# Double blocks with one PSUM tile per bank, gate and value half products in turns, and one listed order for blocks 1 to 8

## The chip, the cores and the metric

The kernel runs on one core of one Trainium2 chip. The engines named below are PE (matrix multiply), PEld (its weight loads), DVE (vector), ACT (scalar activations and copies), POOL (GpSimd) and SP, whose queue issues nearly all DMAs. Every engine works through its own instructions in their order and stops at one whose inputs or room are not there yet. The metric is the device time in microseconds of one execution, the median of several runs.

## The reference

```python
def _attn_ref(q, k, v):                 # (8, 8, 576, 64): batch, heads, positions, head size
    scores = scale * np.matmul(q, k.transpose(0, 1, 3, 2))
    mask_local = (rel >= 0) & (rel < stride)                       # stride 32, heads 0..3
    mask_strided = (rel >= 0) & (pos[None, :] % stride == pos[:, None] % stride)   # heads 4..7
    ...
    attn = np.exp(scores)
    attn = attn / (np.sum(attn, axis=-1, keepdims=True) + 1e-09)
    return np.matmul(attn, v).astype(np.float32)

def _moe_ref(x, w_gate, w_val, w_out):  # x (4608, 512), w_gate and w_val (512, 1536), w_out (1536, 512)
    gate = 1.0 / (1.0 + np.exp(-(x @ w_gate)))
    val = x @ w_val
    return (gate * val @ w_out).astype(np.float32)
```

The attention's output, its heads side by side, is the `x` of the gated layer.

## The kernel before

**Blocks.** The 4608 tokens are nine blocks of 512: for each of the 8 batches the first 512 positions (blocks 0 to 7), and the last 64 of all batches together (block 8). Attention is done in pieces, four for each batch: local heads and strided heads, two times two. A piece is a row of small matmuls for the scores (`score`), mask, maximum, subtraction (`soft`), `expo` on ACT, sum and scaling (`norm`), eight 32-row transposes on DVE (`turn_blocks`), and small matmuls with the values (`weigh`), whose result is copied out of PSUM (`split_high`, `split_low`, `keep_raw`, `keep_rest`). The pieces of batches 2 to 7 are done while the gated layer of earlier blocks runs. Tiles of a piece (`qk`, `vv`, `sb`, `mx`, `pt`) are there once, so one piece is in work at a time.

**The gated layer.** The 1536 inner columns are 12 groups `f` of 128. All float32 values are split into a high and a low part, and each product is three matmuls (high by high, high by low, low by high). For blocks 0, 1 and 2 a group is 12 matmuls of 128x128 by 128x512 for the gate (`g`), 12 for the value (`v`), sigmoid on ACT, product and the two parts on DVE and ACT, and 12 matmuls for the output (`glu_out`), which accumulate over the 12 groups in four banks.

**Double blocks.** Blocks 3 and 4, 5 and 6, 7 and 8 are done in twos (`superblock`, L653), with a scheme of seven products in place of eight. A pair of groups `q` has seven half products for the gates (G1 to G7) and seven for the values (V1 to V7), six matmuls each (L695). Products 1, 6, 7 and 4 are added up in one bank ("a", `to = a`), and after 1, 6 and 7 ACT copies the running sum out (L713) before the next may be added. Products 2, 5 and 3 go to the other bank ("d"), which DVE adds to the copies (L721). Sigmoids follow on ACT (L723, L728), products on DVE (L725, L731), and the hidden values of the second block are kept. Then the output products of the second block run alone, while the seven combinations of the next two blocks' inputs are built (`build_x`: POOL differences, an ACT cast and a DVE subtraction for each). The combinations of the weights are made once, in block 1 (`sum_sets`: six POOL instructions, ACT cast, DVE subtraction, two DMAs), kept in DRAM (`sets`), and come back through a ring of tiles with room for twelve half products (`load_group`).

**PSUM.** Eight banks: `g` and `v` of one bank each, `a`, `o0` and `o1` of two banks each. In double blocks 3 and 7 the gates use `g` and `v`, the values the two halves of the one tile `a`; in double block 5 the gates use the two halves of `o0` and the values those of `o1` (L654). Scores go to `g` and `v` and the values' products of a piece to `a`, or the other way round.

**Order.** Block 0 is listed by hand for all engines (`ORDER`, under `tc.manual_schedule()`). For blocks 1 to 8 only PE has the order in which the program is written (`tc.manual_schedule(engines={PE})`); a planner orders DVE, ACT, POOL and SP by what is ready in its own model of time. PE's order in a pair of groups is `SOFAR` or a variant of it:

```python
SOFAR = "G1 G2 G6 G5 G7 V1 V2 G4 G3 V6 V5 V7 A V4 V3 B"
END = "G1 G2 G6 G5 G7 V1 V2 G4 G3 V6 V5 V7 A Xg V4 Sg V3 B"
```

A and B are the output products of earlier groups, X and S the values and the scores of attention pieces.

Of the kernel before, what the change touches and what calls it, by code (L numbers as in the profile page):

```python
# [52 lines left out]
SOFAR = "G1 G2 G6 G5 G7 V1 V2 G4 G3 V6 V5 V7 A V4 V3 B"  # L53
EARLY = "G1 Xv G2 Sv G6 G5 G7 V1 V2 G4 G3 V6 V5 V7 A Xg V4 Sg V3 B"
MIDDLE = "G1 G2 G6 G5 G7 V1 V2 G4 G3 V6 Xg V5 Sg V7 A V4 V3 B"
FIRST = "G1 G2 G6 Xv G5 Sv G7 V1 V2 G4 G3 V6 V5 V7 A V4 V3 B"
END = "G1 G2 G6 G5 G7 V1 V2 G4 G3 V6 V5 V7 A Xg V4 Sg V3 B"
PLANS = {3: [EARLY, MIDDLE, FIRST] * 2, 5: [END] * 4 + [SOFAR] * 2, 7: [SOFAR] * PAIRS}

# [26 lines left out]
y10 l11.1 X13 s11 a11.2 g11.1 H13 b11.2 L13 R13 w11.2 O10 m11 u11.2 l11.2 x11 y11  # L86
"""
# [6 lines left out]
def attention_then_glu(ctx, tc, qk_l, qk_s, v_l, v_s, w_all, consts, out):  # L94
# [79 lines left out]
    def pair(b, step, space):  # L174
# [52 lines left out]

        def soft():
            sc = todo["soft"]
            prob, row, by_row = rows()  # L230
            if local:
                to = tiles["sb"][:, : 2 * ns * kk].rearrange("p (j n) -> p j n", j=2)
                for j, x in enumerate(sc):
                    heads = to[:, j : j + x.shape[1]]
                    nc.vector.tensor_tensor(heads, x, mask_l.broadcast_to([P, x.shape[1], ns * kk]), op=ALU.add)
            else:
                for j in range(2):
                    sv = sc[j % len(sc)][:, j // len(sc)].rearrange("p (t k) -> p t k", k=kk)
                    nc.vector.tensor_tensor(prob[:, j * ns : (j + 1) * ns], sv, mask_s.broadcast_to([P, ns, kk]), op=ALU.add)  # L239
            nc.vector.tensor_reduce(row, prob, axis=AX.X, op=ALU.max)  # L240
            nc.vector.tensor_tensor(prob, prob, by_row, op=ALU.subtract)
# [5 lines left out]
        def norm():  # L247
            prob, row, by_row = rows()
            nc.vector.tensor_reduce(row, prob, axis=AX.X, op=ALU.add)
            nc.vector.tensor_scalar_add(row, row, 1e-9)  # L250
            nc.vector.reciprocal(row, row)
            nc.vector.tensor_tensor(prob, prob, by_row, op=ALU.mult)

# [13 lines left out]
        def turn_blocks():  # L267

            tiles["pt"] = pt = space.tile([P, 2 * SS * QB], F32, tag="pt", name=f"pt{b}_{step}")
            src, dst = (x[:, : 2 * ns * QB].rearrange("p (t k) -> p t k", k=QB) for x in (tiles["sb"], pt))  # L270
            for n in range(P // LB):
                for h in range(2):
                    to, rows, col = (n // 2 * 2 + h) * LB, n * LB, n % 2 * LB
                    nc.vector.transpose(dst[to : to + LB, :, col : col + LB], src[rows : rows + LB, :, h * LB : (h + 1) * LB])  # L274
# [76 lines left out]
        def keep_rest():  # L351
# [6 lines left out]
            L=split_low, R=keep_rest, K=keep_raw,  # L358
        )

    def banks(tag, name):
        if tag in "gv":
            return [ps.tile([P, BANK], F32, tag=tag, name=name)]
        two = bank(tag, name)
        return [two[:, :BANK], two[:, BANK:]]

    def bank(tag, name):
        return ps.tile([P, 2 * BANK], F32, tag=tag, name=name)
# [63 lines left out]
    def glu_val(k, f, v=None):  # L432
        if v is None:
            v = ps.tile([P, BANK], F32, tag="v", name=f"v{k}_{f}")
            products(v, k, f, 1)
        e = hs[k, f]
        t = work.tile([P, TB], F32, tag="t", name=f"t{k}_{f}") if k == 0 else e
        hh, hl = parts_tiles(k, f)
        def high():
            nc.scalar.copy(hh, t)  # L440

        def low():
            nc.vector.tensor_tensor(hl, t, hh.bitcast(F32), op=ALU.subtract)

        nc.vector.tensor_tensor(t, e, v, op=ALU.mult)  # L445
        if k == 0:
            return high, low
        high(), low()
# [33 lines left out]
    def glu_out(k, *fs):  # L482

        if fs[0] == 0:
            acc[k] = [x for n in ("agv" if k in (4, 5, B) else ("o0", "o1")) for x in banks(n, f"o{k}_{n}")]
        for i in (0, 2, 1, 3) if k == B else range(NTT):
# [15 lines left out]
    ps = ctx.enter_context(tc.tile_pool(name="ps", bufs=1, space=bass.MemoryType.PSUM))  # L502
    dram = ctx.enter_context(tc.tile_pool(name="dram", bufs=1, space=bass.MemoryType.DRAM))
# [4 lines left out]
    pairs = {(b, p): pair(b, p, first if b == 0 and p % 2 else work) for b in range(2) for p in range(4)}  # L508
    products_of = {}
    parts = {}  # L510

    def step(what):

        kind, of = what[0], what[1:]
        if kind in "QVZSFENTPXHLR":
# [6 lines left out]
            pairs[b, p][kind](*args)  # L522
# [36 lines left out]
    sets = {}  # L559
# [3 lines left out]

    def spare(tag, name, dt):
        return work.tile([P, 4, P], dt, tag=tag, name=name)

    def plain_sets(q):
        sets[q] = dram.tile([P, 2 * 7, 2, 2, P], F32, name=f"sets{q}")
        for i in range(2):
            for n, w in ((0, wh), (1, wl)):  # L570
                a, b = (w[f][i].bitcast(F32).rearrange("p (k c m) -> p k c m", k=2, c=2) for f in (2 * q, 2 * q + 1))
                tc.keep_in_program_order(nc.sync.dma_start(sets[q][:, 7 * i : 7 * i + 2, n], a))
                tc.keep_in_program_order(nc.sync.dma_start(sets[q][:, 7 * i + 2, n], b[:, 1]))

    def sum_sets(q, i, c):
        n = (q * 2 + i) * 2 + c
        u = spare(("t", "h0")[n % 2], f"sum{q}_{i}_{c}", F32)
        for at, f in ((0, 2 * q), (2, 2 * q + 1)):
            nc.gpsimd.tensor_tensor(u[:, at : at + 2], part(wh[f][i], c), part(wl[f][i], c), op=ALU.add)
        for to, x, y, op in ((3, 2, 3, ALU.add), (2, 0, 2, ALU.subtract), (0, 3, 0, ALU.subtract), (1, 1, 0, ALU.subtract)):  # L580
            nc.gpsimd.tensor_tensor(u[:, to], u[:, x], u[:, y], op=op)
        h = spare("l0", f"sumh{q}_{i}_{c}", F32R)
        nc.scalar.copy(h, u)
        nc.vector.tensor_tensor(u.bitcast(F32R), u, h.bitcast(F32), op=ALU.subtract)
        nc.sync.dma_start(sets[q][:, 7 * i + 3 : 7 * i + 7, 0, c], h.bitcast(F32))
        nc.sync.dma_start(sets[q][:, 7 * i + 3 : 7 * i + 7, 1, c], u)

    units = [(k, q, u) for k in SUPER for q in range(PAIRS) for u in SOFAR.split() if u not in "AB"]
    groups, ring, left = [], {}, {}
    while sum(len(g) for g in groups) < len(units):  # L590
# [286 lines left out]
```

## Time and profile before

| | us |
|---|---|
| median of 3 runs | 1135.92 |
| lowest and highest of them | 1131.89, 1137.14 |
| the profiled execution: its time | 1141.66 |
| the profiled execution: first to last instruction (span) | 1139.8 |

The mean granted clock of TensorE over the span was 0.96 of full speed. In the views, an instruction's row gives its line, engine, what it writes and reads, and behind "idle before" how long its engine had nothing to do and what ended that. PE's and PEld's rows are two sides of the same work. A matmul's record lasts longer than the distance to the next one, since matmuls are pipelined.

### The profile page before, as it was taken

The numbers are of one execution on the slowest core, as the hardware profiler recorded it, in microseconds if no ns is written. First come the engines' busy times: TensorE is split into PE (matmuls) and PEld (weight loads), VectorE is DVE, ScalarE is ACT, GpSimd is POOL, SyncE is SP. The second block draws the span as 40 slices with busy tenths as digits, with TensorE's granted clock in tenths as the row PEclk, the third lists the DMA queues.
The fourth block names the chain that finished last, engine by engine and source line by source line (L and its number), as shares of the span: only waits on it lengthen the run. The fifth ranks groups of instructions, "written<-read, shape, count | busy, mean of one in ns | idle before, by whom it ended". The sixth has DMA issues, their size and how long they took to land.

```text
span 1139.8 us, 18423 instructions
## 1 busy us (share of the span) xinstructions
PE 985.1 (86%) x7624; PEld 772.5 (68%) x7624; DVE 604.6 (53%) x981; ACT 429.7 (38%) x754; POOL 122.9 (11%) x188
## 2 busy tenths in 40 slices
PE   5998988788799887799889898779788998999998
PEld 4786777667578665577667686556556786777776
DVE  6877846555666685567546752544323633222242
ACT  4877743323433343344333532223222422222221
POOL 0000044575200111000000120000000300000000
PEclk9998999998898897999999999899899999999999
DMA  7665645666512143555445404344333315434311
GB/s 253 205 198 175 190 161 176 203 199 185 166 55 72 55 137 108 179 189 174 141 129 170 148 19 143 115 138 126 94 109 113 109 44 153 137 112 148 110 37 37
DMA packets 85027, 154.13 MB, mean 135 GB/s; under 512 B 5840, under 2 KB 40016, under 8 KB 84944
## 3 DMA queue, kind: packets, MB, share of 16 engines
q1 hardware_dynamic: 83024, 146.72, 40.7%
q10 hardware_dynamic: 1920, 6.24, 1.7%
q8 instruction: 60, 0.98, 0.4%
q14 instruction: 23, 0.19, 0.1%
HBM read 121.48 MB, written 31.46 MB: 134 GB/s over the span
## 4 chain that ended last, share of the span: by engine, by line
PE 46%; DVE 12%; ACT 7%; issue 1%; DMA 0%; POOL 0%; ACTq 0%; DVEq 0%
PE V_a L695 9%; PE o_o L455 8%; PE G_o L695 6%; PE G_g L695 5%; PE V_o L695 4%; PE o_a L455 4%; DVE pt L274 4%; PE G_v L695 3%; PE o_v L455 2%; PE o_g L455 2%; DVE e L721 1%; DVE h L731 1%; ACT e L723 1%; PE x L305 1%; ACT h L713 1%
## 5 line engine op out<-in xcount | busy, mean ns | idle before, releaser
L455 PE MATMUL o_o<-w,hh 128*128 128x512 f32 x576 | 179.2, 392 | 0.0
L695 PE MATMUL V_a<-xs,ring 128*128 128x512 f32 x504 | 133.8, 404 | 31.7 <-DVE h L731 9.8
L695 PEld LDWEIGHTS V_a<-xs,ring 128*128 128x128 f32 x504 | 91.9, 189 | 65.9 <-ACT hid L713 14.3
L455 PEld LDWEIGHTS o_o<-w,hh 128*128 128x128 f32 x576 | 107.8, 189 | 23.1
L418 PE MATMUL g<-xh,w 128*128 128x512 f32 x256 | 95.2, 433 | 27.1 <-DVE sb L239 12.6
L455 PE MATMUL o_o<-w,hl 128*128 128x512 f32 x288 | 112.3, 390 | 0.0
L274 DVE STREAM_TRANSPOSE pt<-sb 32x320 f32<-32x320 f32 (+1 forms) x192 | 102.9, 536 | 3.2
L695 PE MATMUL G_o<-xs,ring 128*128 128x512 f32 x252 | 74.9, 442 | 28.8 <-DVE e L721 15.6
L418 PE MATMUL v<-xh,w 128*128 128x512 f32 x256 | 88.9, 407 | 4.2 <-DVE e L445 4.1
L695 PEld LDWEIGHTS G_o<-xs,ring 128*128 128x128 f32 x252 | 51.0, 211 | 50.2 <-DVE e L721 18.2
L418 PEld LDWEIGHTS g<-xh,w 128*128 128x128 f32 x256 | 53.0, 207 | 42.5 <-DVE sb L239 13.6
L695 PE MATMUL V_o<-xs,ring 128*128 128x512 f32 x252 | 66.3, 402 | 10.8 <-ACT h L713 4.3
L695 PE MATMUL G_g<-xs,ring 128*128 128x512 f32 x288 | 74.3, 393 | 0.0
L695 PE MATMUL G_v<-xs,ring 128*128 128x512 f32 x216 | 58.7, 409 | 8.1 <-DVE e L721 8.1
L695 PEld LDWEIGHTS V_o<-xs,ring 128*128 128x128 f32 x252 | 46.1, 190 | 26.6 <-ACT h L713 6.8
L455 PEld LDWEIGHTS o_o<-w,hl 128*128 128x128 f32 x288 | 54.1, 188 | 12.1 <-DVE hl L738 0.4
L695 PEld LDWEIGHTS G_g<-xs,ring 128*128 128x128 f32 x288 | 54.0, 189 | 12.3 <-ACT e L713 0.6
L418 PEld LDWEIGHTS v<-xh,w 128*128 128x128 f32 x256 | 50.3, 197 | 16.7 <-DVE e L445 5.7
L723 ACT ACTIVATE e<-e 128x512 f32<-128x512 f32 x54 | 34.1, 632 | 72.9 <-DVE e L721 72.8
L199 POOL MEMSET sb<- 128x120 f32 x16 | 3.2, 200 | 527.3 <-DVE pt L274 397.1
L721 DVE TENSOR_TENSOR e<-e,G_v 128x512 f32<-128x512 f32 x36 | 24.6, 684 | 61.1 <-PE G_v L695 31.9
L418 PE MATMUL g<-xl,w 128*128 128x512 f32 x128 | 54.1, 422 | 0.0
(137 smaller groups left out, 1666.4 us busy)
## 6 DMA issues: line engine op xcount, KB each, us to landing
ring<-sets SPq DMA_DIRECT2D x126, 512.0 KB, 3.8
raw<-in_w_all SPq DMA_DIRECT2D x36, 512.0 KB, 4.3
qk<-in_qk_s SPq DMA_DIRECT2D x14, 599.0 KB, 5.5
vv<-in_v_l SPq DMA_DIRECT2D x13, 640.0 KB, 4.8
qk<-in_qk_l SPq DMA_DIRECT2D x14, 592.0 KB, 5.0
out<-ob SPq DMA_DIRECT2D x32, 256.0 KB, 2.0
sets<-w SPq DMA_DIRECT2D x24, 256.0 KB, 3.2
sets<-sumh SPq DMA_DIRECT2D x24, 256.0 KB, 2.4
```

Of the source, the lines that this page charges most:

```text
L199: nc.gpsimd.memset(sb[:, : 2 * ns * QB].rearrange("p (t k) -> p t k", k=QB)[:, :, GS:], 0.0)
L274: nc.vector.transpose(dst[to : to + LB, :, col : col + LB], src[rows : rows + LB, :, h * LB : (h + 1) * LB])
L305: nc.tensor.matmul(at_bank(r, (u * per + g) * m, (u * per + g + 1) * m)[j * D : (j + 1) * D], v[rows, (u * per + g) * P + j * D : (u * per ...
L418: nc.tensor.matmul(o, w, x, start=first and n == 0, stop=last and n == len(todo) - 1)
L455: nc.tensor.matmul(acc[k][i], h[:, i * P : (i + 1) * P], w, start=f == 0 and n == 0, stop=f == NF - 1 and n == 2,)
L695: nc.tensor.matmul(to, w[:, (wi * 2 + c) * P : (wi * 2 + c + 1) * P], x[xi][:, c], start=p in "125" and c == j == 0, stop=c == 1 and j == ...
L713: nc.scalar.copy(got[m, p], a)
L721: nc.vector.tensor_tensor(x, x, d, op=ALU.add)
L723: nc.scalar.activation(x, x, AF.Sigmoid)
L731: nc.vector.tensor_tensor(x, got["G", "4"], a, op=ALU.mult)
```

## The change

All instructions of blocks 1 to 8 are listed, for all engines, in one string `REST_ORDER`, whose entries a table `STEPS` maps to small functions; the plans, `begin_attention`, `scores`, `out_next` and `superblock` go. `ORDER` and block 0 stay. The larger functions are cut into steps (mask, maximum, subtraction and so on) that the list can place one by one. Besides the order:

- The two-bank tile `a` exists during block 0 only. After it, `a0` and `a1` are tiles of one bank each. In all three double blocks the gates use `g` and `v`, the values `a0` and `a1`, and `o0` and `o1` hold the outputs of blocks 1, 2, 3, 5 and 7; those of 4, 6 and 8 are in `g`, `v`, `a0`, `a1`.
- The half products come in the order G1 V1 G2 V2 G6 V6 G5 V5 G7 V7 G4 V4 G3 V3. A ring load brings the gate's and the value's set of one product together.
- Score and value matmuls of a piece stand between pairs of groups; pieces 18 and 19 are taken up in the output stage of block 4 and not in the double block.
- The weight sums are spread over blocks 1 and 2; every other cast has a tile of its own (`ost`).
- A new ACT instruction, `expo_first`, computes an exponential of one column ahead of each piece's `expo`.
- The second of the four input differences runs on DVE and not on POOL. An output row tile's eviction (`e`) and store (`d`) are steps of their own.

```diff
-SOFAR = "G1 G2 G6 G5 G7 V1 V2 G4 G3 V6 V5 V7 A V4 V3 B"
...
+REST_ORDER = """
+LQ0 g1.0 pa0.0.0 LV0 pb0.0.0 pl0 v1.0 s1.0 pa0.0.1 o0.11 pb0.0.1 m1.0 e0.0 x1.0 d0.0 e0.1 y1.0 d0.1 S0.0 LQ1 M0.0 M0.1 D0 g1.1 A0 U0 E0 v1.1 N0 s1.1
+W0 e0.2 e0.3 g1.2 d0.2 m1.1 d0.3 B0.0 x1.1 y1.1 v1.2 B0.1 s1.2 B0.2 ph0.0.0.1 ph0.0.1.0 B0.3 o1.0 m1.2 Z1 pw0.0.0 x1.2 y1.2 pd0.0.0 pw0.0.1 X0.0
...
+ph3.1.1.0 M6.1 A6 D6 U6 pb4.0.0 pl4 g2.3 xh3.0.2 pw3.1.1 E6 xl3.0.2 pd3.1.1 ph4.0.0.1 N6 v2.3 W6 s2.3 B6.0 B6.1 oh2.2.0 B6.2 B6.3 m2.3 Z7 X6.0 pw4.0.0
...
+M14.0 M14.1 D14 A14 U14 G3.2.1 E14 N14 V3.2.1 c3.2.0.1 W14 G3.2.2 r17 c3.2.1.1 B14.0 V3.2.2 B14.1 ad3.2.0.2 G3.2.6 r18 ad3.2.1.2 sg3.2.2 B14.2 V3.2.6
+B14.3 c3.2.0.6 G3.2.5 c3.2.1.6 mu3.2.2 Z15 x3.4 V3.2.5 y3.4 G3.2.7 r19 V3.2.7 c3.2.0.7 ad3.2.0.7 G3.2.4 r20 c3.2.1.7 sg3.2.7 ad3.2.1.7 V3.2.4 mu3.2.7
+sg3.2.4 G3.2.3 r21 mu3.2.4 x3.5 V3.2.3 ad3.2.0.3 y3.5 sg3.2.3 o3.3 r22 ad3.2.1.3 mu3.2.3 X14.0 S15.0 LV15 H14 R14 o3.4 LQ16 M15.0 M15.1 D15 A15 U15
...
+o4.8 x4.10 y4.9 y4.10 X19.1 x4.11 y4.11 S20.1 LV20 H19 o4.9 xh5.1.3 xd5.1.1 LQ21 R19 M20.0 xd5.1.2 xh5.1.6 M20.1 A20 D20 xh5.1.7 xl5.1.6 ob4 xl5.1.7
+xd5.1.3 U20 e4.0 xl5.1.3 xh5.1.4 d4.0 E20 xl5.1.4 e4.1 N20 d4.1 e4.2 G5.0.1 d4.2 W20 B20.0 V5.0.1 c5.0.0.1 e4.3 B20.1 G5.0.2 d4.3 r40 c5.0.1.1 B20.2
...
+"""
...
+        def expo_first():
+            mx = tiles["mx"]
+            nc.scalar.activation(mx[:, 14:15], ident[:, :1], AF.Exp)
...
+    def one_bank(tag, name):
+        return (ps if tag in "gv" else ps_b).tile([P, BANK], F32, tag=tag, name=name)
 
     def bank(tag, name):
-        return ps.tile([P, 2 * BANK], F32, tag=tag, name=name)
+        return (ps_a if tag == "a" else ps).tile([P, 2 * BANK], F32, tag=tag, name=name)
...
+    first_banks.close()
+    ps_b = ctx.enter_context(tc.tile_pool(name="ps_b", bufs=1, space=bass.MemoryType.PSUM))
...
+        (nc.vector if n == 1 else nc.gpsimd).tensor_tensor(t, x, y, op=ALU.subtract)
...
+    def half_product(k, q, m, p):
+        if p == 1:
+            two[m, 0] = one_bank("ga"[m] + "0" * m, f"p{m}{k}_{q}")
+        if p == 2:
+            two[m, 1] = one_bank("va"[m] + "1" * m, f"d{m}{k}_{q}")
+        to = two[m, int(p in (2, 5, 3))]
+        w = ring[k, q, str(p)][:, m]
...
+    STEPS = dict(
+        g=gate, v=val, o=glu_out, oh=lambda k, f, h: glu_out(k, f, half=(h,)), ob=lambda k: glu_out(k, NF - 2, NF - 1),
+        s=lambda k, f: sigmoid(k, f, products_of[k, f, 0]), m=lambda k, f: gated(k, f, products_of[k, f, 1]), x=split_high_h, y=split_low_h,
+        e=evict, d=store, LQ=load_queries, LV=lambda n: piece[n]["V"](), Z=lambda n: piece[n]["Z"](), S=score, M=masks,
...
+        pl=plain_sets, pa=sum_words, pb=sum_parts, ph=sum_high, pw=sum_low, pd=store_sums, r=load_group,
+        G=lambda k, q, p: half_product(k, q, 0, p), V=lambda k, q, p: half_product(k, q, 1, p), c=keep_sum, ad=add_sum, sg=gate_sigmoid,
+        mu=gate_times, xd=diff, xh=set_high, xl=set_low, z=rest_raw,
+    )
+    with tc.manual_schedule():
+        for what in REST_ORDER.split():
+            kind = what.rstrip("0123456789.")
+            STEPS[kind](*(int(n) for n in what[len(kind) :].split(".") if n))
```

In the list, A, U, E, N, W and B are a piece's maximum, subtraction, exponential, sum, scaling and a quarter of its transposes; H, L and R copy its result out of PSUM; `c` is the copy of a running sum, `ad` DVE's addition, `sg` a sigmoid, `mu` a product, `x` and `y` the high and low part of hidden values; `oh` is half of an output group, `ob` two groups at once.

More of the change, by code (lines that the diff above doesn't have):

```diff
@@ L507, in attention_then_glu @@
     left_over(0)
-    pairs = {(b, p): pair(b, p, first if b == 0 and p % 2 else work) for b in range(2) for p in range(4)}
+    firsts = {(b, p): pair(b, p, first if b == 0 and p % 2 else work) for b in range(2) for p in range(4)}
     products_of = {}
-    parts = {}
     def step(what):
@@ L557, in attention_then_glu, with load_queries, score, masks @@
                 left_over(1)
-    sets = {}
+    first_banks.close()
+    ps_b = ctx.enter_context(tc.tile_pool(name="ps_b", bufs=1, space=bass.MemoryType.PSUM))
+    todo = [(b, p) for b in range(BY_PE, B) for p in range(4)]
+    piece = {}
+    def load_queries(n):
+        piece[n] = pair(*todo[n], work)
+        piece[n]["Q"]()
+    def score(n, late):
+        if late:
+            piece[n]["S"](bank("o1", f"s{n}"))
+        else:
+            piece[n]["S"](*(one_bank(t, f"s{n}_{t}") for t in "gv"))
+    def masks(n, j):
+        if piece[n]["local"] and j == 0:
+            piece[n]["Z"]()
+        piece[n]["M"](j)
+    def values(n, late):
+        if late:
+            piece[n]["X"](bank("o0", f"x{n}"))
+        else:
+            piece[n]["X"](*(one_bank(t, f"x{n}_{t}") for t in ("a0", "a1")))
+    def high_of(n):
+        b, p = todo[n]
+        if p == 0:
+            (x_tiles if b < SUPER[0] else raw_tile)(b)
+        if b < SUPER[0]:
+            piece[n]["H"]()
+        else:
+            piece[n]["K"](x_raw[b])
+    def rest_of(n):
+        b, p = todo[n]
+        if p == 0:
+            left_over(b)
+        piece[n]["R"]()
+    def gate(k, f):
+        products_of[k, f, 0] = one_bank("g", f"g{k}_{f}")
+        products(products_of[k, f, 0], k, f, 0)
+    def val(k, f):
+        products_of[k, f, 1] = one_bank("v", f"v{k}_{f}")
+        products(products_of[k, f, 1], k, f, 1)
+    def evict(k, i):
+        give_out(k, i)
+    def store(k, i):
+        nc.sync.dma_start(out[k * S + i * P : k * S + (i + 1) * P], given[k, i])
+    sets, sums, sums_h = {}, {}, {}
     def part(w, c):
         return w.bitcast(F32).rearrange("p (k c m) -> p k c m", k=2, c=2)[:, :, c, :]
-    def spare(tag, name, dt):
-        return work.tile([P, 4, P], dt, tag=tag, name=name)
     def plain_sets(q):
@@ L585, in sum_sets @@
         nc.sync.dma_start(sets[q][:, 7 * i + 3 : 7 * i + 7, 0, c], h.bitcast(F32))
         nc.sync.dma_start(sets[q][:, 7 * i + 3 : 7 * i + 7, 1, c], u)
[L588 to L592 removed]
+    duos = [(k, q, p) for k in SUPER for q in range(PAIRS) for p in USE]
```

517 lines of the change are left out of this document (234 added, 283 removed).

## The prediction

> **What bounds the kernel now.** I read the page first.
>
> ```profile
> span 1139.8 us, 18423 instructions
> PE 985.1 (86%) x7624; PEld 772.5 (68%) x7624; DVE 604.6 (53%) x981; ACT 429.7 (38%) x754; POOL 122.9 (11%) x188
> L695 PE MATMUL V_a<-xs,ring 128*128 128x512 f32 x504 | 133.8, 404 | 31.7 <-DVE h L731 9.8
> L695 PE MATMUL G_o<-xs,ring 128*128 128x512 f32 x252 | 74.9, 442 | 28.8 <-DVE e L721 15.6
> L418 PE MATMUL g<-xh,w 128*128 128x512 f32 x256 | 95.2, 433 | 27.1 <-DVE sb L239 12.6
> ```
>
> PE leads, no other engine passes 53%, and PE's idle time stands before first products of a kind, ended by DVE or ACT. Busy is no measure of PE's need here, because records overlap and a throttled matmul counts as busy. So I asked for busy time by stage: block 0, block 1, block 2, double block 3 with output 4, double block 5 with output 6, double block 7 with output 8; then a dense stretch, one pair of score and value matmuls, and the second part of block 0.
>
> ```profile
> core 0: us, PE busy (x) PEld busy (x) DVE busy (x) ACT busy (x) POOL busy (x), PEclk, DMA share, GB/s
> 0.00:153.04 153.04, 131.24 (x1444) 105.83 (x1445) 116.80 (x208) 104.21 (x196) 2.01 (x9) 0.97 0.63 204
> 153.04:291.83 138.79, 113.81 (x1002) 90.17 (x1000) 74.80 (x123) 45.61 (x74) 83.98 (x146) 0.96 0.58 178
> 291.83:437.40 145.57, 129.91 (x1408) 104.80 (x1409) 98.14 (x168) 56.06 (x98) 10.33 (x11) 0.89 0.32 103
> 437.40:685.36 247.96, 215.56 (x1782) 167.13 (x1781) 153.09 (x246) 98.55 (x168) 14.44 (x15) 0.97 0.43 137
> 685.36:933.92 248.56, 209.00 (x1202) 157.61 (x1201) 101.18 (x150) 73.19 (x128) 12.16 (x9) 0.95 0.34 109
> 933.92:1139.80 205.88, 185.61 (x793) 146.93 (x791) 60.55 (x90) 52.10 (x90) 0.00 (x0) 1.00 0.35 108
> 901.70:933.50 31.80, 31.80 (x141) 26.06 (x140) 17.86 (x21) 10.65 (x19) 8.77 (x6) 1.00 0.09 32
> ...
> 324.63:326.43 1.80, 1.80 (x125) 1.65 (x124) 0.00 (x0) 0.85 (x7) 0.00 (x0) 1.00 0.00 0
> ...
> 46.34:153.04 106.70, 100.67 (x885) 81.10 (x884) 83.48 (x147) 77.38 (x140) 1.42 (x3) 0.97 0.60 186
> ```
>
> The dense stretch gives the price of a matmul: 31.80 us by 141 is 0.2255 us. So a group of 12 costs 2.71 us and a half product of six 1.35. A piece's matmuls take 1.80 us; I add 0.3 for changing over twice, an estimate, and use 2.1.
>
> **What PE needs.** The matmuls do not change. A single block has 36 groups, 432 matmuls, 97.4 us. A double block with its output has 6 x 14 half products and 24 groups, 792 matmuls, 178.6 us. With pieces where the list puts them (4.5, 8, 8, 4, 0 pairs), and 4.5 us from the last matmul to the end:
>
> - block 1: 97.4 + 9.4 = 106.8 of 138.79, lost 32.0
> - block 2: 97.4 + 16.8 = 114.2 of 145.57, lost 31.4
> - double block 3: 178.6 + 16.8 = 195.4 of 247.96, lost 52.6
> - double block 5: 178.6 + 8.4 = 187.0 of 248.56, lost 61.6
> - double block 7: 178.6 + 4.5 = 183.1 of 205.88, lost 22.8
>
> The losses are 200.4 us, and 939.4 is left as a floor with block 0's 153.0. The last matmul ends 4.5 us before 1139.80:
>
> ```profile
> 1134.90 0.39 PE L455 MATMUL o_v<-w,hl 128*128 128x512 f32 x1
> ```
>
> **The change part by part.** *One tile per bank, products in turns.* The timeline of double block 5 shows two kinds of stall:
>
> ```profile
> 697.31 0.58 ACT L713 COPY h<-V_o 128x512 f32<-128x512 f32 x1 [0.77 <-PE V_o L695]
> 697.95 1.66 PE L695 MATMUL V_o<-xs,ring 128*128 128x512 f32 x6 [0.68 <-ACT h L713]
> ...
> 719.50 4.65 DVE L274 STREAM_TRANSPOSE pt<-sb 32x384 f32<-32x384 f32 x8
> 724.18 0.69 DVE L721 TENSOR_TENSOR e<-e,G_o 128x512 f32<-128x512 f32 x1
> 724.90 0.63 ACT L723 ACTIVATE e<-e 128x512 f32<-128x512 f32 x1 [4.99 <-DVE e L721]
> 724.92 2.93 PE L695 MATMUL G_o<-xs,ring 128*128 128x512 f32 x6 [4.59 <-DVE e L721]
> ```
>
> At 697 V2 writes the other half of the two-bank tile and still waits until ACT has copied V1. V1 and V2 have no bank in common, so the wait belongs to the tile. At 724 PE waits for an addition that the planner put behind eight transposes, and 2.93 us for the next six matmuls is the lowered clock. In the new order, V1, G2 and V2 (4.06 us) stand between G1 and G6; the copy of 0.58 and the addition of 0.69 fit. The closest pair is G7 to G4, with V7's 1.35 us for the copy. Double block 7 has no pieces, so its 22.8 are nearly all of this kind: I keep 3 (switches, and the entry from output 6). In double block 5 I keep 8 of 61.6: DVE has 101.18 us of work there, 54% of 187, and the list puts additions ahead of transposes.
>
> *The list in blocks 1 and 2.* Before, the planner's order of DVE makes PE wait like this in block 1:
>
> ```profile
> 254.34 0.62 ACT L583 CAST sumh<-sum 128x512 fp32r<-128x512 f32 x1 [4.45 <-POOL sum L581]
> 254.99 0.81 DVE L584 TENSOR_TENSOR sum<-sum,sumh 128x512 fp32r<-128x512 f32 x1 [4.37 <-DMA sets<-w]
> 258.98 0.49 DVE L239 TENSOR_TENSOR sb<-s_g,cst 128x324 f32<-128x324 f32 x1
> 259.52 0.79 PE L418 MATMUL g<-xh,w 128*128 128x512 f32 x1 [6.37 <-DVE sb L239]
> ```
>
> A weight sum from POOL is late, ACT waits 4.45 us for it, DVE 4.37 behind ACT, the mask of a piece stands behind, and `g` stays full. The list spreads the 24 sums over two blocks, 15 in block 1, so POOL's 83.98 us there (24 sums of 3.5) fall to about 52, and the masks come directly behind the scores. What is queued behind each new place of a sum is a piece's DVE chain; PE's X waits for it. The only measure of a listed order in this kernel is block 0: 6.0 of 106.70 us idle with DVE at 78%. Block 1 will have DVE at (74.80 - 6.7) / 106.8, 64%; I keep 9 of 32.0.
>
> In block 2 the chain itself decides. Its steps in rows:
>
> ```profile
> L240 DVE TENSOR_REDUCE mx<-sb 128x10 f32<-128x640 f32 (+1 forms) x12 | 9.8, 819 | 0.2
> L241 DVE TENSOR_TENSOR sb<-sb,mx 128x640 f32<-128x640 f32 (+1 forms) x12 | 10.7, 894 | 0.4
> L245 ACT ACTIVATE sb<-sb 128x640 f32<-128x640 f32 (+1 forms) x12 | 8.9, 743 | 14.5 <-DVE sb L241 14.4
> L249 DVE TENSOR_REDUCE mx<-sb 128x10 f32<-128x640 f32 (+1 forms) x12 | 9.9, 824 | 13.0 <-ACT sb L245 13.0
> L252 DVE TENSOR_TENSOR sb<-sb,mx 128x640 f32<-128x640 f32 (+1 forms) x12 | 10.2, 847 | 0.4
> L274 DVE STREAM_TRANSPOSE pt<-sb 32x320 f32<-32x320 f32 (+1 forms) x96 | 51.5, 536 | 1.8
> L443 DVE TENSOR_TENSOR hl<-e,hh 128x512 fp32r<-128x512 f32 x24 | 17.3, 723 | 12.0 <-ACT hh L440 11.7
> L443 DVE TENSOR_TENSOR hl<-t,hh 128x512 fp32r<-128x512 f32 x12 | 8.2, 686 | 0.3 <-ACT hh L440 0.3
> L584 DVE TENSOR_TENSOR sum<-sum,sumh 128x512 fp32r<-128x512 f32 x24 | 18.0, 749 | 44.5 <-ACT sumh L583 39.6 <-DMA sets<-w 4.4
> ```
>
> Two masks at 0.49, then 0.82, 0.89, 0.74, 0.82, 0.85 and 8 x 0.536 are 9.4; the two short steps of the sum are under an addition each and I take 0.4 for both, and 0.4 for handovers: 10.2 us. Between scores and values the list has, in three rounds of block 2, only a group, a gate, a value and half a group, 9.5 us, in one 10.8, in the others 13.5 or more. DVE also does 2 to 3 us of other work in a short round, a part of it beside the exponential. PE waits 1 to 2.5 us in four rounds, some 8, and each wait beside small matmuls can cost clock (the granted clock is 0.89 here), some 2 us each, 8 again; with 2 for the rest I keep 18 of 31.4.
>
> *Double block 3.* Two of its eight pieces move to output 4.
>
> ```profile
> 652.12:685.36 33.24, 33.24 (x146) 26.88 (x145) 19.07 (x21) 12.41 (x21) 9.02 (x7) 1.00 0.08 32
> ```
>
> Output 4 is now PE alone, with DVE 19.07 of 33.24. Two pieces bring 2 x 9.1 us, two input differences from POOL, at the addition's 0.69, 1.4: DVE 38.7 against PE's 33.2 + 4.2 = 37.4. DVE becomes the bound there, and its evictions of output 4, ahead of G2 of double block 5, come late. I keep 7 for this and 7 for the double block: 14 of 52.6.
>
> *What costs nothing.* 24 extra exponentials of one column, at ACT's nearest rows 0.2 to 0.7 us, 5 to 17 us on an engine that is busy 38%; they only bring the table load forward. The ring's loads:
>
> ```profile
> ring<-sets SPq DMA_DIRECT2D x126, 512.0 KB, 3.8
> ```
>
> Still 126 of 512 KB: one in 2.71 us of products, landing in 3.8, asked for four or more double products ahead (10.8 us). SP now has them in the list's order beside loads of pieces and stores; if a store held them by more than 7 us, PE would wait for the rest.
>
> **Sum.** Kept: 9 + 18 + 14 + 8 + 3 = 52. Span 939.4 + 52 = 991; the time lies 1.9 above the span (1141.66 to 1139.8), 993. The profiled execution is 5.7 over the median of the runs, a part of which is its clock; I take 990 for the median. As to bounds: only the chain's 8 us kept gives 949; blocks 1 and 2 as now give the first rival.
>
> **The rivals.**
>
> *Blocks 1 and 2 gain nothing, 1026.* Nine sums move beside the pieces of block 2: 31 us of POOL, 9 x 0.75 = 6.7 of DVE. If DVE and POOL hold each other up, DVE's 98.14 + 6.7 + 31 = 136 and the chain's waits leave block 2 at 145 and block 1 with its stalls: 990 + (32.0 - 9) + (31.4 - 18) = 1026. Against it: the same subtraction takes 686 ns in block 0 and 723 where POOL was busy 60% of block 1, so a neighbour costs some 60 ns and not a POOL instruction. The Trainium skill, "SBUF — State Buffer", section "Who interferes with whom", says that a DVE instruction with two SBUF inputs and a GpSimd instruction that reads SBUF exclude each other for a whole instruction. By that rule this rival would be the likelier one; the 37 ns between the two rows do not bear it out. Chance 0.15.
>
> *The turns hide less, 1037.* If ACT is in a sigmoid or an exponential when G7 or V7 ends, the copy comes after V7's 1.35 us: about 1.3 us twice in each of 18 pairs, 47 us. For it: ACT's work, 52.10 us in double block 7 or some 8 in a pair, comes in bursts. Against it: the list has the copies first. Chance 0.09. That the change doesn't do what it says, the wait not being the tile's, would cost little, since PE no longer asks for the other half at once.
>
> *Nearly the floor, 955.* The list's order fits the chip, no clock is lost, and only 17 is kept. Chance 0.12.
>
> *Slower, 1143 or more.* The list fixes DVE and ACT behind POOL's sums whether they are late or not. If each of the 24 sums costs PE the 6.37 us of the row above, 990 + 153 = 1143; it decides from 6.1 us a sum, in blocks 1 and 2. Against it: 15 sums need POOL for 52 us of block 1's 107, so there is room. Chance 0.04.
>
> **How the numbers follow.** Forecast 990, in its own range 970 to 1015, chance 0.60. The range 962 to 1045 takes in the first two rivals and leaves out most of the floor case and the slow one. Within 0.5% of before is what a measurement can't tell from no change; I give it 0.01, slower 0.03, faster 0.96.
>
> **What would show it.** In double block 7 PE's idle time before V products should vanish and the stage take about 186 us. Double block 5 should lose most, to some 195. In block 2 PE should wait for `pt` before X in the short rounds, with a clock under 1.00, and DVE should fill output 4. Wrong would be: PE waiting for the ring's DMAs, waits of several us for POOL on DVE, or a granted clock that falls once PE is dense.

## The result and the profile after

The changed kernel takes 948.24 us (median, 944.96 to 949.55), the kernel before 1136.53 beside it: a ratio of 0.834, 95% interval 0.830 to 0.838. The forecast was 990 us, with 962 as the lower end of its range. The direction was right, the size was not.

From the page after, the span, the busy times and two groups of half products, to be laid beside the first rows of the prediction:

```profile
span 947.8 us, 18546 instructions
PE 919.4 (97%) x7624; PEld 755.6 (80%) x7624; DVE 609.9 (64%) x991; ACT 429.8 (45%) x783; POOL 120.1 (13%) x182
L762 PE MATMUL p<-xs,ring 128*128 128x512 f32 x864 | 204.6, 389 | 0.0
L762 PE MATMUL d<-xs,ring 128*128 128x512 f32 x648 | 155.6, 389 | 0.0
```

The number of matmuls is the same. PE's idle time fell from 154.7 us (1139.8 - 985.1) to 28.4, and its busy time by 65.7. A part of that is the clock, since a throttled matmul has a longer record (0.95 in double block 5 before, 1.00 after). Not all of it is: in double block 7 the clock was 1.00 before and after, and the busy time fell by 5.9. The half products, which had 31.7 and 28.8 us of idle time ahead of them in two of their groups, have none. The other engines do nearly what they did.

This is the busy time by stage (block 0; blocks 1 and 2; double blocks 3, 5, 7, each with its output). PE's granted clock stands behind POOL's column:

```profile
core 0: us, PE busy (x) PEld busy (x) DVE busy (x) ACT busy (x) POOL busy (x), PEclk, DMA share, GB/s
0.00:151.18 151.18, 129.84 (x1444) 103.79 (x1445) 116.75 (x208) 103.51 (x196) 1.61 (x9) 0.99 0.62 201
151.18:379.63 228.45, 226.07 (x2422) 186.15 (x2420) 177.99 (x294) 104.74 (x192) 96.96 (x155) 1.00 0.58 180
379.63:576.51 196.88, 196.76 (x1770) 162.51 (x1768) 148.32 (x241) 91.80 (x170) 11.83 (x12) 1.00 0.54 172
576.51:763.57 187.06, 187.06 (x1202) 154.66 (x1200) 106.22 (x161) 77.23 (x136) 9.73 (x8) 1.00 0.46 145
763.57:947.80 184.23, 179.68 (x793) 148.46 (x791) 60.62 (x89) 52.53 (x89) 0.00 (x0) 1.00 0.38 117
```

From block 1 on PE is busy in all but the last 4.5 us and some 2.5 before. These are the waits left before the end, by the view of PE's waits from block 1 on:

```profile
PE x_a L399 <- DVE pt L368: 1.1, 3, 0.6
PE g L478 <- DVE sb L310: 0.6, 1, 0.6
PE g L478 <- DVE sb L315: 0.6, 1, 0.6
```

The timeline of double block 7 shows what the turns do, where before V2 stood behind the copy of V1:

```profile
786.69 1.52 PE L762 MATMUL p<-xs,ring 128*128 128x512 f32 x6
786.94 0.59 ACT L791 COPY e<-p 128x512 f32<-128x512 f32 x1 [4.14 <-PE p L762]
...
788.05 2.88 PE L762 MATMUL d<-xs,ring 128*128 128x512 f32 x12
...
788.30 0.59 ACT L791 COPY h<-p 128x512 f32<-128x512 f32 x1 [0.77 <-PE p L762]
```

V1 runs at 786.69 while ACT copies G1, and G2 and V2 run from 788.05 while it copies V1. No row of PE has a wait.

### The profile page after: what moved, and what is told of

Read it like the earlier page. It is cut to its first block, busy times and chain, and to the rows that moved or that the text cites. A ratio compares the mean times of both kernels' runs of the same rounds, so it can differ in the third digit from the quotient of the medians.

```text
span 947.8 us, 18546 instructions
## 1 busy us (share of the span) xinstructions
PE 919.4 (97%) x7624; PEld 755.6 (80%) x7624; DVE 609.9 (64%) x991; ACT 429.8 (45%) x783; POOL 120.1 (13%) x182
## 4 chain that ended last, share of the span: by engine, by line
PE 84%; DVE 6%; DMA 5%; ACT 3%; issue 1%; SPq 0%; ACTq 0%; DVEq 0%
PE p L762 21%; PE o L509 17%; PE d L762 15%; PE v L478 8%; PE g L478 7%; PE o_a L509 5%; DMA raw<-in_w_all 4%; PE x_a L399 2%; PE o_g L509 2%; PE o_v L509 2%; DVE pt L368 1%; PE s_v L295 1%; PE s_g L295 1%; PE s L295 1%; PE x L399 1%
## 5 line engine op out<-in xcount | busy, mean ns | idle before, releaser
L762 PE MATMUL p<-xs,ring 128*128 128x512 f32 x864 | 204.6, 389 | 0.0
L762 PEld LDWEIGHTS p<-xs,ring 128*128 128x128 f32 x864 | 162.2, 188 | 33.7
L509 PE MATMUL o<-w,hh 128*128 128x512 f32 x576 | 180.4, 394 | 0.0
L762 PE MATMUL d<-xs,ring 128*128 128x512 f32 x648 | 155.6, 389 | 0.0
L762 PEld LDWEIGHTS d<-xs,ring 128*128 128x128 f32 x648 | 121.6, 188 | 25.3
L509 PEld LDWEIGHTS o<-w,hh 128*128 128x128 f32 x576 | 106.3, 188 | 22.7
L509 PE MATMUL o<-w,hl 128*128 128x512 f32 x288 | 112.2, 390 | 0.0
L791 ACT COPY e<-p 128x512 f32<-128x512 f32 x54 | 31.7, 587 | 114.9 <-PE p L762 114.7
L509 PEld LDWEIGHTS o<-w,hl 128*128 128x128 f32 x288 | 54.1, 188 | 11.8 <-DVE hl L502 0.3
L690 POOL TENSOR_TENSOR sum<-sum 128x128 f32<-128x128 f32 x96 | 51.4, 535 | 7.4
L478 PE MATMUL v<-xl,w 128*128 128x512 f32 x128 | 50.7, 396 | 0.0
L502 DVE TENSOR_TENSOR hl<-hid,hh 128x512 fp32r<-128x512 f32 x36 | 26.9, 750 | 34.3 <-ACT hh L498 34.1
```

Of the source, the lines that this page charges most:

```text
L478: nc.tensor.matmul(o, w, x, start=first and n == 0, stop=last and n == len(todo) - 1)
L502: nc.vector.tensor_tensor(hl, whole_h.pop((k, f)), hh.bitcast(F32), op=ALU.subtract)
L509: nc.tensor.matmul(acc[k][i], h[:, i * P : (i + 1) * P], w, start=f == 0 and n == 0, stop=f == NF - 1 and n == 2,)
L762: nc.tensor.matmul(to, w[:, (wi * 2 + c) * P : (wi * 2 + c + 1) * P], x[xi][:, c], start=p in (1, 2, 5) and c == j == 0, stop=c == 1 and j ...
L791: nc.scalar.copy(x, two[m, 0])
```

## The experiments

Theory A: the gain comes mainly from the listed order of the engines other than PE. Theory B: mainly from single-bank tiles and turns. The first five runs go by engine. In their table block 0 ends with the first gate product of block 1, and each double block begins with its first half product.

**Listed order for some engines only.** Tiles, turns and instructions stay. The names of the engines are shortened here.

```diff
-    with tc.manual_schedule():
+    with tc.manual_schedule(engines={PE}):                    # e1
+    with tc.manual_schedule(engines={PE, DVE}):               # e2
+    with tc.manual_schedule(engines={PE, Activation}):        # e5
+    with tc.manual_schedule(engines={PE, DVE, Activation}):   # e6
+    with tc.manual_schedule(engines={PE, DVE, Activation, Pool}):   # e12
```

> The changed kernel, tiles, turns, PE's order and every instruction kept, but the listed order binds PE alone; the planner orders DVE, ACT, POOL and SP again in blocks 1 to 8. Theory A (most of the 188 us comes from the listed order of the other engines: what is late no longer stands ahead of what PE waits for): 1050 to 1110 us, with waits of several us on DVE and ACT in blocks 1 and 2 and a granted clock under 1.00 in block 2. Theory B (most of it comes from one tile per bank and the turns, which hide an order that is not ideal): 950 to 975 us, and what is lost lies in blocks 1 and 2.

> As the run before, with the listed order for PE and DVE; the planner orders ACT, POOL and SP. If DVE's order is what made PE wait (its row in the profile of before names DVE ahead of most idle time): within 10 us of the changed kernel, 945 to 960. If DVE only passed on what ACT, POOL or SP had late: halfway or less, 1000 or more.

> The changed kernel with the listed order for PE and ACT; the planner orders DVE, POOL and SP. With PE alone listed the double blocks were already at most 10 us above the changed kernel each, and blocks 0 to 2 took 439 us, as before the change; there ACT stood 42 us behind POOL's sums, with sigmoids behind it. If ACT's order is what made PE wait in blocks 1 and 2: blocks 0 to 2 near 385 to 395 us and in all 955 to 985. If ACT and DVE pass the same delay on to each other, so that one in order does not help: blocks 0 to 2 still over 415 us, in all 1000 or more.

> The changed kernel with the listed order for PE, DVE and ACT; the planner orders POOL and SP. If the stall came from sums, casts and stores standing ahead of a piece's chain on DVE and ACT: 945 to 960 us. If POOL, which waited 114 us for the stores of sums with PE and DVE listed, or SP's order of loads is its root, the sums stay late and now hold DVE and ACT fixed behind them: 990 or more, with waits on POOL sums in the rows.

> The changed kernel with the listed order for all engines but SP, whose loads and stores the planner orders. With POOL and SP left to the planner it took 957.8 us in the profile, 10 us more, all of them in blocks 0 to 2, where POOL waited 75 us for the stores of sums. If SP's order (loads of queries and values ahead of the stores that free the sums' buffers) is the rest: 954 to 960 us. If POOL's own order is: 946 to 951.

The ratio is to the kernel before, measured beside each run; the stages are those of the profiled execution.

| listed | median us | ratio to before, 95% | block 0 | blocks 1 and 2 | double 3 | double 5 | double 7 |
|---|---|---|---|---|---|---|---|
| before | 1136.5 | 1 | 153.0 | 284.4 | 248.0 | 248.6 | 205.9 |
| PE (e1) | 1022.5 | 0.900 (0.897 to 0.903) | 156.9 | 282.4 | 206.4 | 190.8 | 184.2 |
| PE, DVE (e2) | 1003.3 | 0.884 (0.880 to 0.889) | 162.5 | 277.1 | 197.6 | 187.1 | 184.2 |
| PE, ACT (e5) | 991.9 | 0.870 (0.866 to 0.873) | 158.4 | 258.9 | 202.6 | 187.4 | 184.2 |
| PE, DVE, ACT (e6) | 956.5 | 0.839 (0.836 to 0.842) | 160.0 | 229.7 | 196.9 | 187.1 | 184.2 |
| all but SP (e12) | 955.3 | 0.839 (0.836 to 0.841) | 156.5 | 229.3 | 196.9 | 187.1 | 184.2 |
| all (after) | 948.2 | 0.834 (0.830 to 0.838) | 151.2 | 228.5 | 196.9 | 187.1 | 184.2 |

Blocks 1 and 2 of e1, from its windows:

```profile
156.85:439.29 282.44, 244.18 (x2422) 194.98 (x2421) 175.92 (x300) 119.10 (x204) 92.96 (x156) 0.95 0.37 115
```

e1's 1022 lies between the ranges of the two theories, and each theory holds in one part of the kernel. With PE alone listed, blocks 1 and 2 gain 2 us, and the three double blocks already gain 41.6 + 57.8 + 21.7 = 121 of their 134 us. The list of the other engines brings 54 us in blocks 1 and 2, 13 in the double blocks and 6 in block 0. In blocks 1 and 2 neither engine's order does it alone: DVE's listed order brings 5 us, ACT's 24, both together 53. So e2 fell into its second case, where DVE only passes on what is late elsewhere, and e5's 992 lies in neither of its ranges. In e1 and e2 the planner also parts the early exponentials from their pieces: ACT loads a table 66 times, where it does so 52 times when its order is listed. What this costs there was not tried alone.

Why DVE's order is not enough shows in e2's timeline, where ACT is in the planner's order:

```profile
260.65 0.62 ACT L695 CAST sumh<-sum 128x512 fp32r<-128x512 f32 x1 [8.27 <-POOL sum L690]
...
264.08 0.74 ACT L334 ACTIVATE sb<-sb 128x648 f32<-128x648 f32 x1
264.86 0.83 DVE L338 TENSOR_REDUCE mx<-sb 128x12 f32<-128x648 f32 x1 [8.55 <-ACT sb L334]
...
268.57 0.60 ACT L486 ACTIVATE e<-g 128x512 f32<-128x512 f32 x1
269.22 0.79 PE L478 MATMUL g<-xh,w 128*128 128x512 f32 x1 [6.08 <-ACT e L486]
```

Two casts of weight sums stand ahead of the piece's exponential on ACT, and the first waits 8.27 us for POOL. DVE waits 8.55 us for the exponential, the sigmoid comes after it, and PE waits 6.08 us for the bank `g`. An in-order queue hands its delay to the next engine, so the chain runs as late as its worst-ordered queue.

POOL and SP together are the last 8 to 10 us, and these are not lost in blocks 1 and 2, where e6 and e12 take 229.7 and 229.3 us against 228.5. They are lost in block 0, though its own list is the same in all runs. It ends between 156.5 and 162.5 us in the five runs in which the planner orders SP, and between 146.6 and 151.8 in the eight with all engines listed. The planner lets SP copy the plain weights to `sets` early: all 44 of these copies, which the list puts in blocks 1 and 2, are issued before 145 us in the five runs, and none in the changed kernel. The first of them and the window of block 0 in e12:

```profile
16.60 0.38 SPq L678 DMA_DIRECT2D sets<-w  x1
0.00:156.45 156.45, 134.06 (x1444) 106.61 (x1445) 116.78 (x208) 103.68 (x196) 1.37 (x9) 0.97 0.77 250
```

The DMA engines are busy 0.77 of the time there, where it is 0.62 after. By the ratios SP's order costs some 5 us (0.8385 for e12, 0.8335 for e10 and e11 in the same comparison). That the copies hold up block 0's own loads is likely; no run moved them alone. e12's time is in the range of its expectation, but the reason named there, stores of sums in blocks 1 and 2, is not what its stages show. POOL's order by itself shows nothing.

**The value banks as one tile again.**

The values of pieces and half of an output sum become one tile as well; the gates keep their single banks (both are left out of this cut).

```diff
-        if p == 1:
-            two[m, 0] = one_bank("ga"[m] + "0" * m, f"p{m}{k}_{q}")
-        if p == 2:
-            two[m, 1] = one_bank("va"[m] + "1" * m, f"d{m}{k}_{q}")
+        if m == 1 and p == 1:
+            x = both(f"p{k}_{q}")                  # one tile of two banks
+            two[1, 0], two[1, 1] = x[:, :BANK], x[:, BANK:]
...
```

> The changed kernel with the two banks of the value products, of the values of pieces and of half an output sum as one tile again; the turns and the list are kept. Theory: the wait is the tile's; with the turns V2 has G2's 1.35 us and V4 has G4's beside the copy and the addition before it, so about 0.3 to 1 us a pair of groups is left: 953 to 966 us. Rival: the turns hide the tile's wait wholly, 946 to 950. Second rival: single tiles carry most of the gain in the double blocks, 1000 or more.

959.46 us, ratio 0.845 (0.841 to 0.848). Its windows of the double blocks:

```profile
378.62:581.14 202.52, 199.72 (x1769) 161.77 (x1768) 149.39 (x241) 91.10 (x166) 11.73 (x12) 1.00 0.52 167
581.14:772.25 191.11, 189.75 (x1201) 153.95 (x1200) 106.22 (x161) 77.19 (x134) 9.72 (x8) 1.00 0.45 142
772.25:958.90 186.65, 181.86 (x793) 147.84 (x791) 60.62 (x89) 53.12 (x90) 0.00 (x0) 1.00 0.38 116
```

The double blocks lose 5.6 + 4.1 + 2.4 = 12.1 us, 0.67 for each of 18 pairs of groups. That is the theory's range: the wait is the tile's, and the turns hide most of it. In both runs no two products that follow each other use the same bank; what differs is the tile. The timeline shows one such wait, ahead of V4 (both halves of the tile are called `p` here):

```profile
786.46 0.59 ACT L798 COPY hid<-p 128x512 f32<-128x512 f32 x1 [0.77 <-PE p L769]
787.07 0.69 DVE L803 TENSOR_TENSOR hid<-hid,p 128x512 f32<-128x512 f32 x1 [0.67 <-ACT hid L798]
787.81 1.22 PEld L769 LDWEIGHTS p<-xs,ring 128*128 128x128 f32 x6 [0.46 <-DVE hid L803]
```

V4 adds to the first half, which ACT has copied out by 787.05. It still waits until DVE's addition, which reads the second half, ends at 787.76.

**Without turns.** The half products in the order of before, every copy, addition and product directly behind what it needs; single banks and the list stay.

```diff
-... G3.1.1 U13 V3.1.1 c3.1.0.1 E13 G3.1.2 r11 c3.1.1.1 N13 V3.1.2 W13 ad3.1.0.2 G3.1.6 ...
+... G3.1.1 c3.1.0.1 U13 G3.1.2 ad3.1.0.2 sg3.1.2 E13 G3.1.6 c3.1.0.6 N13 G3.1.5 W13 G3.1.7 ...
```

> The changed kernel with the half products of the double blocks in the order of before (G1 G2 G6 G5 G7 V1 V2 G4 G3 V6 V5 V7 V4 V3), each copy, addition, sigmoid and product directly behind the half product that it needs, and the ring's loads where their slot is free; one tile per bank and the list are kept. Theory: single banks leave one pair without cover, V7 to V4, some 0.8 us in each of 18 double groups, and G1 to G6 and V6 to V7 have 1.35 us for a copy of 0.58: 960 to 970 us. Rival (the turns carry the gain): each of four handovers costs 0.7 us or more, 50 us, 1000 or more. Second rival (order of the engines is all): 946 to 952.

1022.43 us, ratio 0.900 (0.897 to 0.904), but PE waited 28.9 us of it for the ring's loads. A gate's and a value's matrix came in one load, and with the value's product far behind the gate's its room came free late. So the loads were changed as well:

```diff
-    duos = [(k, q, p) for k in SUPER for q in range(PAIRS) for p in USE]
+    duos = [(k, q, u) for k in SUPER for q in range(PAIRS) for u in UNITS.split()]   # G1 G2 G6 G5 G7 V1 ...
```

> The run without turns again, with the ring's loads as before: pairs of matrices in the order in which that order of half products uses them, each asked for as soon as its slot is free. The first run without turns took 1022 us, of which PE waited 29 us for the ring's loads and 12 for the copy ahead of V4 (18 times 0.7). If the loads were the rest: 960 to 975 us, with the 12 us for the copy left. If the order of half products itself costs the time: 1000 or more again.

990.41 us, ratio 0.868 (0.865 to 0.871): between the two cases. Its windows of the double blocks, and the largest row of PE's waits in them:

```profile
380.37:596.24 215.87, 202.31 (x1769) 161.05 (x1768) 147.20 (x241) 92.57 (x172) 12.16 (x12) 1.00 0.49 157
596.24:797.25 201.01, 191.14 (x1202) 153.59 (x1200) 105.45 (x161) 78.36 (x138) 9.64 (x8) 1.00 0.42 135
797.25:987.30 190.05, 181.47 (x793) 148.00 (x791) 60.07 (x89) 52.09 (x89) 0.00 (x0) 0.99 0.37 114
```

```profile
PE p L769 <- ACT hid L798: 19.6, 25, 1.7
```

The turns are worth 19.0 + 13.9 + 5.8 = 39 us here. The row of copies has 25 waits of 0.8 us in the mean, where 18 of 0.7 were expected for V7 to V4; where pieces fill DVE and ACT (double blocks 3 and 5) the loss is 3.3 and 2.4 times that of double block 7. Turns under the planner, or the list without turns, each bring most of the double blocks' gain. Only both bring all of it. Single banks alone, with the planner and without turns, were not tried.

**The chain of a piece, 0.82 us longer, or with the table load in it.** The maximum (`A`) of each piece is taken twice; in the other run the 24 early exponentials (`D`) are left out.

```diff
-g1.1 A0 U0 ...
+g1.1 A0 A0 U0 ...          # e8
-M0.0 M0.1 D0 g1.1 ...
+M0.0 M0.1 g1.1 ...         # e9
```

> The changed kernel with the maximum of each of the 24 pieces taken twice, 0.82 us more in the chain between scores and values. The prediction held that in blocks 1 and 2 and in output 4 this chain is at its edge, which is why it kept 18 us of loss: then four to six short rounds lengthen by about 0.8 us each and a lowered clock comes with them, 952 to 965 us. If the chain has room, as PE's waits of 0.2 to 0.6 us before values suggest in three rounds only: 3 rounds of 0.8, 949 to 951.

> The changed kernel without the 24 early exponentials of one column, so that ACT's table load of 1.28 us stands in the chain between a piece's subtraction and its exponential again. The prediction called them free and the chain in the short rounds of block 2 its edge; twice the maximum (0.82 us more) took 3.8 us in the profile. By the same edge: three short rounds that already wait 0.2 to 0.6 us and three more that twice the maximum brought to the edge, each later by up to 1.28 us: 6 to 8 us, 953 to 957 us. If the table load lies beside DVE's other work there: 0 to 2 us.

e8: 954.09 us, 0.837 (0.833 to 0.840). e9: 951.60 us, 0.835 (0.833 to 0.836). From e8, the largest row of PE's waits, the window of blocks 1 and 2, and a window around the third of the rounds that wait:

```profile
PE x_a L399 <- DVE pt L368: 3.3, 6, 0.7
147.00:382.66 235.66, 230.91 (x2421) 189.12 (x2420) 188.90 (x306) 104.75 (x193) 95.34 (x155) 0.99 0.56 175
352.00:366.00 14.00, 12.72 (x152) 10.43 (x151) 12.19 (x21) 5.05 (x9) 0.20 (x1) 0.76 0.57 169
```

It is the same three rounds of block 2 that wait in the changed kernel, each now twice: 0.9, 1.1 and 1.3 us in place of 0.6, 0.3 and 0.2. So in these three the chain has no room, and in sum most of the 0.82 us comes through; the other rounds have more room than that. Behind the third round the clock was lowered once in this execution. Blocks 1 and 2 take 7.2 us more than after, 235.7 for 228.5, where the five runs that leave the chain alone (e3, e4, e7, e10, e11) have 228.3 to 230.0. The span is only 3.8 us longer, because block 0 happened to end 4 us earlier, and the ratio alone doesn't separate e8 from the changed kernel. So both cases of the expectation hold in part: three rounds, and a lowered clock with them.

e9 shows no cost of the table load: the span is 1.9 us longer, which the ratio doesn't show, blocks 1 and 2 take 229.7 us, and PE waits 1.2 us for `pt` in three rounds, against 1.1. So the load lies beside other work even when it isn't brought forward.

**POOL's work beside DVE, and the second difference.**

```diff
             nc.gpsimd.tensor_tensor(u[:, to], u[:, x], u[:, y], op=op)
+        for _ in range(4):
+            nc.gpsimd.tensor_tensor(spare, cst[:, :P], ident, op=ALU.subtract)    # e11
-        (nc.vector if n == 1 else nc.gpsimd).tensor_tensor(t, x, y, op=ALU.subtract)
+        nc.gpsimd.tensor_tensor(t, x, y, op=ALU.subtract)                         # e10
```

> The changed kernel with four more subtractions of 128x128 from constants on POOL behind each of the 24 sums in blocks 1 and 2, into a tile that nobody reads: some 50 us of POOL work beside DVE, and nothing waits for its result. If DVE and POOL exclude each other for whole instructions (the rival of 1026 us): DVE's subtractions of two SBUF inputs go from 0.69 to 1.0 us or more in the mean, and blocks 1 and 2 lose 10 us or more, 960 to 990. If a neighbour costs some 60 ns, the mean of these rows rises by under 0.1 us and the kernel loses 0 to 4 us.

> The changed kernel with the second input difference of each double block on POOL again (1.5 us there, 0.68 on DVE). Six instructions: if DVE were the bound in output 4, as the prediction had it (38.7 us of DVE against 37.4 of PE), the kernel would win up to 1.4 us or stay; if the differences are a chain on POOL with the double block waiting at its end, it loses about 1 us in each of two double blocks: 948 to 951 us.

e11: 949.82 us, 0.834 (0.832 to 0.835). e10: 951.01 us, 0.834 (0.831 to 0.836). Neither ratio shows an effect. Three groups of DVE in blocks 1 and 2 follow, first after, then in e11 with its added group on POOL (lines are 1 to 3 further down there):

```profile
L699 DVE TENSOR_TENSOR sum<-sum,sumh 128x512 fp32r<-128x512 f32 x24 | 18.8, 796 | 5.0 <-ACT sumh L695 4.7
L502 DVE TENSOR_TENSOR hl<-e,hh 128x512 fp32r<-128x512 f32 x24 | 17.7, 736 | 5.7 <-ACT hh L498 4.8
L491 DVE TENSOR_TENSOR e<-e,v 128x512 f32<-128x512 f32 x24 | 16.5, 687 | 17.3 <-PE v L478 16.5
```

```profile
L693 POOL TENSOR_TENSOR spare<-cst 128x128 f32<-128x128 f32 x96 | 49.5, 515 | 5.6
...
L503 DVE TENSOR_TENSOR hl<-e,hh 128x512 fp32r<-128x512 f32 x24 | 19.0, 790 | 5.6 <-ACT hh L499 4.8
L702 DVE TENSOR_TENSOR sum<-sum,sumh 128x512 fp32r<-128x512 f32 x24 | 17.6, 745 | 15.8 <-ACT sumh L698 15.7
L492 DVE TENSOR_TENSOR e<-e,v 128x512 f32<-128x512 f32 x24 | 16.4, 685 | 13.3 <-PE v L479 11.2 <-ACT e L487 1.4
```

With 49.5 us more of POOL one subtraction of two SBUF tiles rises from 736 to 790 ns in the mean and the other falls from 796 to 745, so the two together take what they took (36.5 and 36.6 us). The product with one input in PSUM stays. For the time of the kernel this is nothing: PE waits 1.1 us for `pt` in both runs.

## Why the prediction was wrong, step by step

**The floor was right, but for 5 us in blocks 1 and 2.** Measured against it: block 0 151.2 for 153.0 (unchanged work), blocks 1 and 2 228.5 for 221.0, double block 3 196.9 for 195.4, double block 5 187.06 for 187.0, double block 7 184.2 for 183.1.

**The step that failed is the sum of the kept losses, 52 us, of which 10 are there, and only 2.5 of these are waits of PE.** By its terms:

| kept in | forecast | measured |
|---|---|---|
| blocks 1 and 2 | 9 + 18 | 7.5 |
| double block 3 with output 4 | 14 | 1.5 |
| double block 5 | 8 | 0.1 |
| double block 7 | 3 | 1.1 |

With block 0 at 1.8 us less than before, the span is 8.4 over the floor. With 8.4 in place of 52 the prediction's own sum gives 946.

- *Block 2's 8 us for `pt`: 1.1 in three rounds.* The chain's length was right: 10.2 us forecast, and in the short round below it takes 10.6 from the first mask at 286.18 to the end of the transposes. What failed is what was added for "2 to 3 us of other work" of DVE: where that work lies decides, by the timeline:

```profile
286.18 0.49 DVE L310 TENSOR_TENSOR sb<-s_g,cst 128x320 f32<-128x320 f32 x1 [0.99 <-PE s_v L295]
...
288.70 0.95 DVE L699 TENSOR_TENSOR sum<-sum,sumh 128x512 fp32r<-128x512 f32 x1
289.57 0.95 DVE L748 TENSOR_TENSOR xs<-xraw,xs 128x512 fp32r<-128x512 f32 x1
290.44 0.81 DVE L338 TENSOR_REDUCE mx<-sb 128x10 f32<-128x640 f32 x1
...
292.60 4.17 DVE L368 STREAM_TRANSPOSE pt<-sb 32x320 f32<-32x320 f32 x8
...
297.41 0.69 DVE L699 TENSOR_TENSOR sum<-sum,sumh 128x512 fp32r<-128x512 f32 x1
```

```profile
286.71 1.28 ACT L330 ACT_TABLE_LOAD   x1
288.01 0.20 ACT L330 ACTIVATE mx<-cst 128x1 f32<-128x1 f32 x1
...
288.81 0.74 ACT L334 ACTIVATE sb<-sb 128x640 f32<-128x640 f32 x1
```

```profile
295.83 0.42 PE L399 MATMUL x_a<-pt,vv 64*64 64x32 f32 x12
296.83 1.07 PE L399 MATMUL x_a<-pt,vv 64*64 64x32 f32 x57 [0.58 <-DVE pt L368]
```

  Two instructions of other work (L699, L748) fill the time in which DVE would wait for the exponential (it ends at 289.55, the row sum begins at 290.44, so 0.9 us is lost). The rest comes behind the transposes, beside PE's X and S. X also begins before the last transposes: its first 12 matmuls run at 295.83, and PE waits only 0.58 us in this round. e8 shows that the prediction was right to see the edge here.
- *The 8 us of lowered clock: none.* The clock is 1.00 from block 1 on. In e1, where PE has single waits of up to 6.5 us in blocks 1 and 2, it is 0.95 there, and in e8 it was lowered once behind a round that waits 1.3 us. The term hung on the waits, and fell with them.
- *Block 1's 9 us, by block 0's idle share.* PE idles 2.4 us in blocks 1 and 2 together (228.45 - 226.07), not 6.0 in 106.70 as in block 0's second part. The other 5 us over the floor are PE's own work there that the floor counted too low. The starts of the matmuls take them apart: one output group of block 0, 2.7 us, stands in block 1 and was counted nowhere; the 876 large matmuls take 0.230 us each and not 0.2255, 4.0 us; and the pieces' small matmuls take 1.7 us less in sum than 2.1 a pair.
- *Double block 3's 14, half of it for DVE as the bound of output 4.* The forecast was 38.7 us of DVE against 37.4 of PE. The window of output 4:

```profile
539.27:576.51 37.24, 37.12 (x390) 30.56 (x388) 34.44 (x58) 14.87 (x32) 6.49 (x5) 1.00 0.29 101
```

  PE's 37.4 was right; DVE has 34.44, 92% of the window, and stays below.
- *Double block 5's 8.* Nothing is left. With the planner's order of DVE the stage takes 190.8 us (e1), with the listed one 187.1 (e2), so DVE's listed order is worth 3.7 of the 61.5 us gained; tiles and turns, with PE alone listed, bring the rest.

**What was right.** That V2's wait belongs to the tile (e3: 12 us if undone, even with turns); that double block 7's 22.8 us were of this kind (e1 regains 21.7 with PE alone listed); that blocks 1 and 2 gain by the list (e1: 2 us without it); that DVE's pieces keep the chain at its edge in short rounds (e8); that the early exponentials and the ring's loads cost nothing. One reading was wrong without touching the sum: the prediction named DVE's order as what made PE wait in block 1, though its own rows begin with ACT's wait for a sum from POOL. By e2 and e5 ACT's order has the larger part.

**The rivals.** "Nearly the floor, 955" came true, at a chance of 0.12 and left outside the range. "Blocks 1 and 2 gain nothing" fell: they gain 56 us (284.4 to 228.5). Its mechanism is there, though, and the prediction dismissed it on a mean. After, the single rows of L699 in blocks 1 and 2 have 686 ns in the mean of the 16 without a POOL instruction beside them. Six have POOL beside them for nine tenths of their length or nearly so: five take 0.95 to 1.27 us, 1157 ns in the mean, and one 0.69 (the round above shows 0.95 at 288.70, and 0.69 without POOL at 297.41). Four such rows of L502 take 0.69 to 0.98 us, 837 ns in the mean. This is the lock that the Trainium skill, "SBUF — State Buffer", section "Who interferes with whom", describes for DVE instructions with two SBUF inputs; the trace agrees in most of these rows and not in all, and L491, with one input in PSUM, stays at 684 ns without POOL and 688 with it. The delay met few instructions, and e11 shows that even 50 us more of POOL change nothing in the time. "The turns hide less" and "Slower" fell: PE waits for no copy and for no sum from block 1 on.

## What to carry to other kernels

A loss that is kept in a forecast needs an instance (which instruction will be late, behind what, by how much); an idle share from another stage, or an engine at 90%, is none. When in-order engines feed each other, an order for one of them only moves the wait to the next, so list all engines of a loop before judging what an order is worth. Compare runs stage by stage: here a stage that no run meant to change, block 0, ended between 146.6 and 162.5 us, and hid or mimicked effects of 4 to 10 us in the whole. Two halves of one tile are one object for waits: give each bank a tile of its own, and put other products between a product and the one that must wait for its copy.

## What the runs showed of the hardware

The delay of DVE beside POOL shows in single rows and less in means: 686 ns alone, 1157 in five of six rows beside POOL, 796 in the mean of all 24. An ACT table load took 1.28 us, and the instruction behind it began at once (286.71 + 1.28, the next row at 288.01). In the changed kernel the granted clock stayed at 1.00 from block 1 on, through all rounds of small matmuls, with no single wait over 0.64 us before the end. In e8 two waits of 0.62 and 0.66 us in one round of small matmuls were followed by a lowered clock, 0.76 over 14 us; in e7 waits of up to 1.7 us between half products went with 1.00, 1.00 and 0.99.
